# Twenty fused tiles instead of twelve in a talking-heads attention with FFN, opening tiles accumulated in parts

## The chip, the core and the metric

One core of one Trainium2 chip runs the whole program. The metric is the device time of one execution in microseconds (us). Engines are named as in the profile: PE is TensorE, DVE is VectorE, ACT is ScalarE, POOL is GpSimd, SP is SyncE.

## What is computed

Batch 8, 12 heads, sequence 448, head size 64. Attention scores are mixed across heads before the softmax (w_pre) and the weights are mixed across heads after it (w_post); the result, 3584 rows of 768, goes through a feed-forward network of width 2048 with a squared ReLU.

```python
scores = scale * np.matmul(q, k.transpose(0, 1, 3, 2))
scores = np.einsum('bhij,hg->bgij', scores, w_pre)
attn = np.exp(scores - max); attn = attn / (sum + 1e-09)
attn = np.einsum('bhij,hg->bgij', attn, w_post)
x = np.matmul(attn, v)            # then rows of all heads side by side
h = np.maximum(x @ w_in, 0.0)
out = h * h @ w_out
```

## The kernel before

**Tiles.** A tile is ten query rows of one batch with all twelve heads, 120 partitions by 448 keys. A batch has 45 tiles, and one loop of steps (L465) works through 360 of them. In step i, `mix` (L369) makes the mixed scores of tile i on PE, ACT takes the exponential with its row sums, DVE the reciprocal, and POOL scales a 120x120 matrix built from w_post by it (`pn`). Four steps later `unmix` (L392) multiplies the exponentials by that matrix, which mixes the heads and transposes at once, and DVE copies the result to SBUF (L403).

**Two ways to mixed scores.** The usual way has three stages. `score_burst` (L320) computes the scores of 128 queries for a few heads, two matmuls for a pair of heads, and ACT and DVE copy them into a buffer S (two of them, each for a block of 128 queries and all heads). `gather` (L349) then lets SP issue a DMA that brings ten queries of all heads onto 120 partitions (buffer G, twelve of them, at most ten steps ahead). One matmul with the matrix `pre` mixes the heads (L381). For batch 0 there is a second way that needs no gather: the *fused* tiles. `mix_queries` (L172) lets DVE multiply the transposed queries by w_pre for each target head, and six accumulating matmuls of 128x448 per tile (L376), one for each pair of heads, give the mixed scores directly. In the kernel before, tiles 0 to 11 are fused, and tiles 12 to 44 come from three score blocks. The mixed queries are kept in three of the four buffers that later hold w_out.

**The start.** q, k and v of batch 0 are loaded in thirds of four heads (L88 to L94, L426). For each third u, `turn_unit` (L181) transposes q with sixteen small PE transposes, DVE copies them (qT), DVE mixes the queries (tiles 0 to 3 first, then 4 to 11), then k is transposed and ACT copies it (kT). Behind the second third stands a burst for two pairs of heads; the other pairs of the first block follow in steps 0 and 1. Gathers begin in step 2.

**The order of the work.** On PE and POOL instructions keep the order of the program; on DVE and ACT a scheduler chooses the order of the queue. All engines work their queues in order. A PSUM tile is one of eight banks, given out dynamically: a matmul that begins a tile waits until the bank's earlier tile has been copied out. Loads are issued by POOL at fixed steps: `KQ_AT` (k and q of batches 1 and 2), `W1_AT` (w_in in six pieces), `W2_AT` (w_out in eight pieces), `V1_AT`. Transposes of the next batch come at the steps of `TURN`. Between mix and unmix, PE takes units of the feed-forward network from a list (`filler`), as many as spread them evenly to the next bound; `EARLY` (L45) says at which step the hidden units of a third of batch 0 are put on that list.

Of the kernel before, what the change touches and what calls it, by code (L numbers as in the profile page):

```python
# [8 lines left out]
BF16 = mybir.dt.bfloat16  # L9
# [5 lines left out]
B, H, S, D = 8, 12, 448, 64  # L15
DMODEL = H * D
DFF = 2048
NPAIR = H // 2
# [3 lines left out]
IQ = 10  # L22
NT = 45
RG = H * IQ
FUSED = 12
FQ = FUSED * IQ
NEAR = 4
STARTS = {0: (FQ, 2 * FQ, S - 128)}
FIRST = {0: (FUSED, 2 * FUSED, 3 * FUSED)}
BURSTS = {0: ([5, 8], [5, 8], [3, 6])}  # L30
for _b in range(1, B):
    STARTS[_b], FIRST[_b], BURSTS[_b] = (0, 128, 256, 384), (0, 13, 26, 39), ([5, 8], [5, 8], [6], [0, 3])
GATHERS_AT = 2
HALF = H // 2
TT = 15
TQ = TT * IQ
# [1 line left out]
AHEAD = 10  # L38
SCALE = 1.0 / 8.0
TURN = {0: (17, 17, 21, 21, 25, 25), 1: (20, 20, 24, 24, 28, 28), B: (1 + LAG,) * 3 + (16 + LAG,) * 3}  # L40
KQ_AT = {1: (5, 7, 9, 11, 13, 15), 2: (52, 54, 56, 58, 60, 62)}
W1_AT = (-1, 1, 3, 18, 21, 24)
W2_AT = (30, 33, 36, 39, 42, 45, 48, 51)
V1_AT = (47, 50, 53)
EARLY = ((21, 0, 0, 2), (32, 0, 2, 4), (38, 1, 0, 4), (52, 2, 0, 4))  # L45
FFN2_AT = 60
MAIN = 3 * 128

# [2 lines left out]
def kernel(  # L51
# [11 lines left out]
    nc = tc.nc  # L63
    P = nc.NUM_PARTITIONS

    consts = ctx.enter_context(tc.tile_pool(name="consts", bufs=1))
# [12 lines left out]
    def stage_tile(name, bufs):  # L79
        return stage.tile([P, H, R, D], BF16, name=name, tag=name, bufs=bufs)  # L80

    def load(t, src, b, h0=0, h1=H):
        nc.gpsimd.dma_start(out=t[0:PR, h0:h1, :, :].rearrange("p h r d -> p h (r d)"),
                            in_=src[b, h0:h1, :, :].rearrange("h (p r) d -> p h (r d)", r=R))

    staged, vs = {}, {}
    staged[0] = (stage_tile("qst", 1), stage_tile("kst", 1))
# [41 lines left out]
    for t in range(3 * P // IQ, NT):  # L129
        n0, n = max(0, 3 * P - IQ * t), min(IQ, S - IQ * t)  # L130
# [29 lines left out]
    for t in ets:  # L160
# [4 lines left out]
    w2 = [wts.tile([P, FT // 4, DMODEL], BF16, name=f"w2_{x}") for x in range(4)]  # L165

    qTs, kTs, xts, h2ts, ats = {}, {}, {}, {}, {}

    qmix = [w2[u][:, :, :].rearrange("p c m -> p (c m)")[:, 0:2 * FQ * H].rearrange(
        "p (y t g i) -> p y t g i", y=2, g=H, i=IQ) for u in range(NPAIR // 2)]  # L170

    def mix_queries(u, t0, t1):  # L172

        for y in range(2):
            qs = qTs[0][:, 2 * u + y, IQ * t0:IQ * t1].rearrange("p (t i) -> p t i", i=IQ)
            nc.vector.tensor_tensor(out=qmix[u][:, y, t0:t1, :, :],
                                    in0=qs.unsqueeze(2).to_broadcast([P, t1 - t0, H, IQ]),
                                    in1=wrep[:, 2 * u + y, :, :].unsqueeze(1).to_broadcast([P, t1 - t0, H, IQ]),
                                    op=ALU.mult)
# [140 lines left out]
    def score_burst(b, blk, pairs):  # L320
# [3 lines left out]
        sb = Sb[(b, blk)]  # L324
        q0 = STARTS[b][blk]
        got = []
# [22 lines left out]
    def gather(s):  # L349

        b, t = s
        g = work.tile([P, S], BF16, name="G", tag="G", bufs=AHEAD + 2)
        x, end = IQ * t, min(IQ * t + IQ, S)
        while x < end:
            blk = x // P if b else min(x // FQ, 3) - 1
            n = min(end, STARTS[b][blk] + P) - x
            o, y = H * (x - IQ * t), x - STARTS[b][blk]
            sb = Sb[(b, blk)]
            dst = g[o:o + H * n, :]
            if blk < 3:  # L360
                nc.sync.dma_start(out=dst, in_=sb[y:y + n, :, :])
            else:
                for c in range(2):
                    nc.sync.dma_start(out=g[o + HALF * n * c:o + HALF * n * c + HALF * n, :],
                                      in_=sb[64 * c + y:64 * c + y + n, 0:HALF, :])
            x += n
        Gs[s] = g

    def mix(s):  # L369
        n = rows_of(s[1])  # L370
        b, t = s
        ps = bank("m_ps")
        fused = b == 0 and t < FUSED
        if fused:
            for p in range(NPAIR):
                nc.tensor.matmul(ps[0:n, 0:S], rhs=kTs[b][:, p, :],  # L376
                                 lhsT=qmix[p // 2][:, p % 2, t, :, :].rearrange("p g i -> p (g i)"),
                                 start=(p == 0), stop=(p == NPAIR - 1))
        else:
            m = pres[max(x for x in pres if x <= t)] if b else pre  # L380
# [42 lines left out]
    blocks = [(b, blk) for b in range(B) for blk in range(len(STARTS[b]))]  # L423
    steps = [(b, t) for b in range(B) for t in range(NT)]
    with tc.manual_schedule(engines={PE, POOL}):
        for x in range(3):  # L426
            load_v(0, x)
        for u in range(NPAIR // 2):
            turn_unit(0, 0, u)
            mix_queries(u, 0, NEAR)  # L430
            mix_queries(u, NEAR, FUSED)
            turn_unit(0, 1, u, nc.scalar.copy)
            if u == 1:
                score_burst(0, 0, [0, 1])
        loads = {}
        ahead = [FUSED]

# [27 lines left out]
        for i in range(-1, end):  # L465
            for f in loads.get(i, []):
                f()
            if i < 0:
                continue
            if i == NT // 2:  # L470
                for (_, n), (t, order) in orders.items():
                    half_pre(n, t, order)
            s0 = steps[i] if i < len(steps) else None
            s1 = steps[i - LAG] if LAG <= i < len(steps) + LAG else None
            if s0:
                b, t = s0
                if t == 0:
                    if b + 1 < B:
                        for x, u in enumerate(turn_units(b + 1)):
                            at_step(i + TURN.get(b, TURN[B])[x], u)  # L480
            early = [x for x in bounds if x > i]
            rest = early[0] - i if early else (1 + LAG - i) % NT + 1
            rest = min(rest, end - i) if i > len(steps) - NT // 2 else rest
            share = sum(w for w, _ in filler) / rest / 2
            now = timed.pop(i, [])
            if s0:
                mix(s0)
            for w, f in now:
                f()
                owed[0] -= w  # L490
            fill(share)
            if s1:
                unmix(s1)
                b1, t1 = s1
                if t1 % TT == TT - 1:
                    for u in av_units(b1, t1 // TT):
                        at_step(i + 3, u)
                if t1 == NT - 1:
                    at_step(i + 3 if b1 else FFN2_AT, (0, lambda b1=b1: filler.extend(ffn_units(b1))))
            if i < 2:  # L500
                score_burst(0, 0, [2 + 2 * i, 3 + 2 * i])
            for _ in range(2 if i >= GATHERS_AT else 0):
                if ahead[0] > min(max(i + AHEAD, 2 * FUSED - 1), len(steps) - 1):
# [46 lines left out]
```

## Time and profile before

| | |
|---|---|
| three timed runs | 600.27, 600.85 and 602.12 us, median 600.85 |
| the profiled execution | 600.99 us, span 599.2 us |
| busy in the span | PE 574.3, DVE 411.7, ACT 380.6, POOL 326.1 us |
| first matmul | 7.12 us |
| fused mix, 72 matmuls of 128x448 (L376) | tiles 0 to 11, steps 0 to 11 |
| mix of a gathered tile (L381) | 348 matmuls of 120x448, mean 358 ns from start to end |
| gathers | 354 DMA issues by SP |
| read from and written to HBM | 45.70 MB, 11.01 MB |

The mean duration of a matmul reaches from its start to its last result; matmuls overlap, so the distance between two starts is shorter than the duration. A name such as `s_ps L332` is the tile that is written and the line in the kernel before; in the changed kernel the line numbers are higher by up to 35.

### The profile page before, as it was taken

To read this page: it belongs to the slowest core of one execution; us is meant where nothing else is said; L and a number is where in the kernel's file an instruction comes from. 1 tells how busy PE (TensorE), PEld (TensorE's weight loads), DVE (VectorE), ACT (ScalarE), POOL (GpSimd) and SP (SyncE) were. 2 spreads that over 40 slices of the span, in tenths; PEclk is the share of its full clock that TensorE was granted. 3 is DMA by queue.
4 is the path that set the end of the run, shared out by engine and by line. 5 is a ranking of instruction groups with operands and counts; after the bars stand their busy time and mean duration, and the time that the engine had idled before them with its cause. 6 is when DMAs were issued, how large, how long until landed. Compare 5 with 4: busy or idle time off the path is not lost.

```text
span 599.2 us, 17220 instructions
## 1 busy us (share of the span) xinstructions
PE 574.3 (96%) x6011; PEld 372.2 (62%) x6011; DVE 411.7 (69%) x1044; ACT 380.6 (64%) x1105; POOL 326.1 (54%) x708
## 2 busy tenths in 40 slices
PE   4979999899999999999999999999999999999996
PEld 3547777566566666566565665666665666666553
DVE  5668769988767777767777777777867667666011
ACT  3757978676876557864776547775677547762410
POOL 5354897362777227862569316792377325761730
PEclk9999999999999999999999999999999999999999
DMA  9898999698569755795458855697544755431003
GB/s 128 141 199 164 191 197 196 128 172 193 100 101 140 145 100 109 121 156 124 98 94 135 151 111 101 113 143 138 109 79 69 133 119 107 84 50 54 27 27 79
DMA packets 88279, 72.28 MB, mean 121 GB/s; under 512 B 6688, under 2 KB 83200, under 8 KB 88192
## 3 DMA queue, kind: packets, MB, share of 16 engines
q1 hardware_dynamic: 50394, 48.16, 36.6%
q0 software_dynamic: 37216, 22.81, 29.3%
q8 instruction: 47, 0.77, 0.5%
q10 hardware_dynamic: 582, 0.21, 0.2%
q14 instruction: 40, 0.33, 0.1%
HBM read 45.70 MB, written 11.01 MB: 95 GB/s over the span
## 4 chain that ended last, share of the span: by engine, by line
PE 81%; DMA 10%; ACT 3%; issue 2%; DVE 1%; POOL 1%; SPq 1%; ACTq 0%; POOLq 0%; DVEq 0%
PE o_ps L295 24%; PE h_ps L251 22%; PE at_ps L401 10%; PE m_ps L381 10%; DMA G<-S 7%; PE ot_ps L209 6%; PE s_ps L332 4%; PE tr_ps L193 3%; ACT e L384 2%; DMA w<-in_moe_w_in_dram 2%; DMA kst<-in_k_dram 1%; ACT S L342 1%; PE m_ps L376 1%; DVE S L344 1%; PE s_ps L338 1%
## 5 line engine op out<-in xcount | busy, mean ns | idle before, releaser
L403 DVE CAST at<-at_ps 112x480 bf16<-112x480 f32 x360 | 228.5, 650 | 73.3 <-PE at_ps L401 72.8
L384 ACT ACTIVATE e<-m_ps 120x448 bf16<-120x448 f32 x360 | 195.5, 547 | 98.8 <-PE m_ps L381 92.4
L388 POOL TENSOR_SCALAR pn<-post,rc 120x120 bf16<-120x120 bf16 x348 | 129.0, 372 | 207.1 <-DVE rc L386 147.6
L251 PE MATMUL h_ps<-xt,w 128*128 128x448 bf16 (+2 forms) x960 | 169.6, 315 | 1.1 <-ACT hr L257 0.6
L295 PE MATMUL o_ps<-w,h 128*128 128x384 bf16 x768 | 138.7, 326 | 0.3 <-ACT S L342 0.2
L401 PE MATMUL at_ps<-pn,e 120*128 120x120 bf16 (+1 forms) x1440 | 135.1, 216 | 0.7 <-POOL pn L388 0.5
L401 PEld LDWEIGHTS <-e 120*128 120x128 bf16 (+1 forms) x1440 | 103.9, 98 | 45.0 <-issue 1.4
L381 PE MATMUL m_ps<-G,pre 120*120 120x448 bf16 x348 | 124.6, 358 | 2.1 <-ACT S L342 1.0
L251 PEld LDWEIGHTS <-w 128*128 128x128 bf16 x960 | 84.6, 98 | 57.7 <-issue 5.6
L262 POOL TENSOR_TENSOR h<-hr 128x384 bf16<-128x384 f32 (+1 forms) x144 | 106.1, 738 | 19.4 <-ACT hr L257 15.6
L257 ACT ACTIVATE hr<-h_ps 128x448 f32<-128x448 f32 (+2 forms) x160 | 75.4, 473 | 52.7 <-PE h_ps L251 35.9
L295 PEld LDWEIGHTS <-h 128*128 128x128 bf16 x768 | 72.8, 98 | 48.2 <-issue 5.5
L344 DVE CAST S<-s_ps 128x448 bf16<-128x448 f32 x159 | 89.2, 615 | 4.2 <-DMA G<-S 2.3
L386 DVE RECIPROCAL rc<-sm 120x1 f32<-120x1 f32 x360 | 57.2, 159 | 45.2 <-ACT e L384 37.3
L342 ACT CAST S<-s_ps 128x448 bf16<-128x448 f32 x171 | 79.8, 546 | 11.9 <-PE s_ps L332 8.4
L384 ACT ACTIVATION_READ_ACCUMULATOR e<-m_ps 120x1 f32 x360 | 74.1, 206 | 0.0
L304 DVE COPY osb<-o_ps 128x384 f32<-128x384 f32 x54 | 30.1, 557 | 46.8 <-PE o_ps L295 46.6
L381 PEld LDWEIGHTS <-pre 120*120 120x120 bf16 x348 | 46.1, 133 | 20.9 <-issue 14.6
L332 PE MATMUL s_ps<-kT,qT 64*128 64x448 bf16 x288 | 41.5, 355 | 5.8 <-ACT S L342 4.4
L209 PE MATMUL ot_ps<-at,v 112*64 112x150 bf16 x1152 | 42.6, 230 | 0.0
L209 PEld LDWEIGHTS <-v 112*64 112x64 bf16 x1152 | 38.3, 110 | 4.9 <-issue 4.9
L215 ACT CAST xt<-ot_ps 128x450 bf16<-128x450 f32 (+1 forms) x48 | 25.5, 533 | 20.4 <-PE ot_ps L209 19.9
(45 smaller groups left out, 288.2 us busy)
## 6 DMA issues: line engine op xcount, KB each, us to landing
G<-S SPq DMA_DIRECT2D x284, 105.0 KB
qst<-in_q_dram POOLq DMA_DIRECT2D x24, 224.0 KB, 5.7
kst<-in_k_dram POOLq DMA_DIRECT2D x24, 224.0 KB, 5.2
v<-in_v_dram POOLq DMA_DIRECT2D x24, 224.0 KB, 6.9
G<-S SPq DMA_DIRECT2D x70, 52.5 KB
w<-in_moe_w_in_dram POOLq DMA_DIRECT2D x6, 512.0 KB, 10.3
w<-in_moe_w_out_dram POOLq DMA_DIRECT2D x8, 384.0 KB, 7.7
out_dram<-osb SPq DMA_DIRECT2D x8, 336.0 KB
```

The costliest lines, as they stand in the source:

```text
L209: nc.tensor.matmul(ps[64 * hh:64 * hh + 64, TQ * y:TQ * y + TQ], lhsT=vs[b][0:PR, g, r, :], rhs=at[0:PR, r, g, :], start=(y == 0 and r == ...
L251: nc.tensor.matmul(ps[:, 0:n], lhsT=w1[ft // 8][:, c2, ft % 8 * 128:ft % 8 * 128 + 128], rhs=xts[b][:, c2, n0:n1], start=(c2 == 0), stop=( ...
L257: nc.scalar.activation(out=hr[:, 0:n], in_=ps[:, 0:n], func=ACT.Relu)
L262: eng.tensor_tensor(out=dst[:, x - o:y - o], in0=hr[:, x - n0:y - n0], in1=hr[:, x - n0:y - n0], op=ALU.mult)
L295: nc.tensor.matmul(ps[:, 0:384], lhsT=lhsT, rhs=w2[ft // 4][:, ft % 4, nt * 384:(nt + 1) * 384], start=(ft == 0), stop=(ft == FT - 1))
L342: nc.scalar.copy(out=sb[:, h, :], in_=ps[:, 0:S])
L344: nc.vector.tensor_copy(out=sb[:, h, :], in_=ps[:, 0:S])
L381: nc.tensor.matmul(ps[0:n, 0:S], lhsT=m[0:n, 0:n], rhs=Gs.pop(s)[0:n, :], start=True, stop=True)
L384: nc.scalar.activation(out=e[0:n, 0:S], in_=ps[0:n, 0:S], func=ACT.Exp, scale=SCALE, accum_out=sm[0:n, 0:1])
L388: nc.gpsimd.tensor_scalar(out=pn[0:n, :], in0=(post_gi if fused else post)[0:n, :], scalar1=rc[0:n, 0:1], scalar2=1.0, op0=ALU.mult, op1=A ...
L401: nc.tensor.matmul(ps[:, RG * r:RG * r + RG], lhsT=e[0:n, PR * r:PR * r + P], rhs=pn[0:n, :], start=True, stop=True)
L403: nc.vector.tensor_copy(out=ats[(b, third)][0:PR, :, :, IQ * tl:IQ * tl + IQ], in_=ps[0:PR, 0:R * RG].rearrange("p (r g i) -> p r g i", r= ...
```

## The change

Twenty tiles are fused instead of twelve. Two score blocks remain in batch 0 (queries 200 to 327 and 320 to 447) instead of three. The mixed queries of tiles 12 to 19 go to three more buffers that are free at that time: the fourth one of w_out, the second one of v and the second one of the FFN's input (`late`); their mixing is written at steps 3, 4 and 5, one third each. For tiles 0 to 4 the six accumulating matmuls are issued in three parts of two (`fused_part`): the part of a third of the heads follows the transposes of the next third's q, and the last part stands in the tile's own step. Thirteen matmuls on a zeroed tile (`still`) stand ahead of the first transposes, two more behind the first k. The first score block moves from the start to steps 0 to 2, gathers begin in step 4, and the steps of some loads and of one `EARLY` entry move. Buffers are computed from the same data, and nothing else of the computation changes.

In the queues of the built program, PE has 86 more rows, the DMA issues of SP are eight fewer, and from about step 39 on all five queues are the same as before. DVE's scheduled queue has the mixing for tiles 12 to 19 at the start: one of the six instructions stands ahead of the second third's mixing, three behind it and ahead of the third q copy, two behind the third third's mixing, and only then come the first reciprocal and the score copies.

```diff
-FUSED = 12
+FUSED = 20
+SOON = 12
-NEAR = 4
-STARTS = {0: (FQ, 2 * FQ, S - 128)}
-FIRST = {0: (FUSED, 2 * FUSED, 3 * FUSED)}
-BURSTS = {0: ([5, 8], [5, 8], [3, 6])}
+NEAR = 5
+STARTS = {0: (FQ, S - 128)}
+FIRST = {0: (FUSED, 32)}
+BURSTS = {0: ([4, 8], [5, 8])}
-GATHERS_AT = 2
+GATHERS_AT = 4
+WARM = (13, 2)
-KQ_AT = {1: (5, 7, 9, 11, 13, 15), 2: (52, 54, 56, 58, 60, 62)}
-W1_AT = (-1, 1, 3, 18, 21, 24)
+KQ_AT = {1: (4, 6, 8, 10, 12, 14), 2: (52, 54, 56, 58, 60, 62)}
+W1_AT = (-1, 1, 3, 15, 17, 19)
-EARLY = ((21, 0, 0, 2), (32, 0, 2, 4), (38, 1, 0, 4), (52, 2, 0, 4))
+EARLY = ((21, 0, 0, 2), (28, 0, 2, 4), (38, 1, 0, 4), (52, 2, 0, 4))
...
+    still_in = consts.tile([P, 512], BF16, name="still_in")
+    nc.vector.memset(still_in[:, :], 0.0)
+    still_out = bank("still_ps")
+
+    def still(n):
+        for _ in range(n):
+            nc.tensor.matmul(still_out[:, :], lhsT=still_in[:, 0:P], rhs=still_in[:, :], start=True, stop=True)
...
+    late = [w2[3][:, :, :].rearrange("p c m -> p (c m)"), stage_tile("v", 2)[:, :, :, :].rearrange("p h r d -> p (h r d)"),
+            ffnp.tile([P, NPAIR, S], BF16, name="xt", tag="xt", bufs=2)[:, :, :].rearrange("p c s -> p (c s)")]
+
+    def mixed(u, y, t0, t1):
+        if t0 < SOON:
+            buf, x = w2[u][:, :, :].rearrange("p c m -> p (c m)"), SOON * y + t0
+        else:
+            buf, x = late[u], (FUSED - SOON) * y + t0 - SOON
+        return buf[:, RG * x:RG * (x + t1 - t0)]
...
+    parts = {}
+
+    def fused_part(t, u):
+
+        if t not in parts:
+            parts[t] = [0, bank("m_ps")]
+        if parts[t][0] > u:
+            return
+        parts[t][0] = u + 1
+        for p in (2 * u, 2 * u + 1):
+            nc.tensor.matmul(parts[t][1][0:RG, 0:S], rhs=kTs[0][:, p, :], lhsT=mixed(u, p % 2, t, t + 1),
+                             start=(p == 0), stop=(p == NPAIR - 1))
...
         if fused:
-            for p in range(NPAIR):
-                nc.tensor.matmul(ps[0:n, 0:S], rhs=kTs[b][:, p, :],
-                                 lhsT=qmix[p // 2][:, p % 2, t, :, :].rearrange("p g i -> p (g i)"),
-                                 start=(p == 0), stop=(p == NPAIR - 1))
+            for u in range(NPAIR // 2):
+                fused_part(t, u)
+            ps = parts[t][1]
...
+        still(WARM[0])
         for x in range(3):
             load_v(0, x)
         for u in range(NPAIR // 2):
             turn_unit(0, 0, u)
             mix_queries(u, 0, NEAR)
-            mix_queries(u, NEAR, FUSED)
+            mix_queries(u, NEAR, SOON)
+            if u:
+                for t in range(NEAR):
+                    fused_part(t, u - 1)
             turn_unit(0, 1, u, nc.scalar.copy)
-            if u == 1:
-                score_burst(0, 0, [0, 1])
+            if u == 0:
+                still(WARM[1])
...
-            if i < 2:
-                score_burst(0, 0, [2 + 2 * i, 3 + 2 * i])
+            if 2 < i < 6:
+                mix_queries(i - 3, SOON, FUSED)
+            if i < 3:
+                score_burst(0, 0, [2 * i, 2 * i + 1])
```

More of the change, by code (lines that the diff above doesn't have):

```diff
@@ L167 @@
     qTs, kTs, xts, h2ts, ats = {}, {}, {}, {}, {}
-    qmix = [w2[u][:, :, :].rearrange("p c m -> p (c m)")[:, 0:2 * FQ * H].rearrange(
-        "p (y t g i) -> p y t g i", y=2, g=H, i=IQ) for u in range(NPAIR // 2)]
+    late = [w2[3][:, :, :].rearrange("p c m -> p (c m)"), stage_tile("v", 2)[:, :, :, :].rearrange("p h r d -> p (h r d)"),
[6 more added lines that the diff above has]
+        return buf[:, RG * x:RG * (x + t1 - t0)]
     def mix_queries(u, t0, t1):
@@ L175, in mix_queries @@
             qs = qTs[0][:, 2 * u + y, IQ * t0:IQ * t1].rearrange("p (t i) -> p t i", i=IQ)
-            nc.vector.tensor_tensor(out=qmix[u][:, y, t0:t1, :, :],
+            nc.vector.tensor_tensor(out=mixed(u, y, t0, t1).rearrange("p (t g i) -> p t g i", g=H, i=IQ),
                                     in0=qs.unsqueeze(2).to_broadcast([P, t1 - t0, H, IQ]),
@@ L354, in gather @@
         while x < end:
-            blk = x // P if b else min(x // FQ, 3) - 1
+            blk = max(y for y, q0 in enumerate(STARTS[b]) if q0 <= x)
             n = min(end, STARTS[b][blk] + P) - x
@@ L371, in mix @@
         b, t = s
-        ps = bank("m_ps")
         fused = b == 0 and t < FUSED
         if fused:
-            for p in range(NPAIR):
-                nc.tensor.matmul(ps[0:n, 0:S], rhs=kTs[b][:, p, :],
-                                 lhsT=qmix[p // 2][:, p % 2, t, :, :].rearrange("p g i -> p (g i)"),
-                                 start=(p == 0), stop=(p == NPAIR - 1))
+            for u in range(NPAIR // 2):
+                fused_part(t, u)
+            ps = parts[t][1]
         else:
+            ps = bank("m_ps")
             m = pres[max(x for x in pres if x <= t)] if b else pre
@@ L499 @@
                     at_step(i + 3 if b1 else FFN2_AT, (0, lambda b1=b1: filler.extend(ffn_units(b1))))
-            if i < 2:
-                score_burst(0, 0, [2 + 2 * i, 3 + 2 * i])
+            if 2 < i < 6:
+                mix_queries(i - 3, SOON, FUSED)
+            if i < 3:
+                score_burst(0, 0, [2 * i, 2 * i + 1])
             for _ in range(2 if i >= GATHERS_AT else 0):
-                if ahead[0] > min(max(i + AHEAD, 2 * FUSED - 1), len(steps) - 1):
+                if ahead[0] > min(max(i + AHEAD, FIRST[0][1] - 1), len(steps) - 1):
                     break
```

## The prediction

> **What bounds the kernel now.** I read the page first: TensorE (PE) is busy nearly all the time, and the chain that ended last is PE's for four fifths.
>
> ```profile
> span 599.2 us, 17220 instructions
> PE 574.3 (96%) x6011; PEld 372.2 (62%) x6011; DVE 411.7 (69%) x1044; ACT 380.6 (64%) x1105; POOL 326.1 (54%) x708
> PEclk9999999999999999999999999999999999999999
> ```
>
> So a change can gain only where PE stands still or runs slowly, and each matmul that it adds costs its full length. Busy shares hide slow matmuls, so I took the starts of all matmuls from the trace and used the median distance from one start to the next as a matmul's price: 189 ns for a fused one (128x448), 192 ns for the mix of a gathered tile, 52 ns for one of an unmix, 190 ns for a pair of score matmuls (they start together). Time minus the sum of prices is loss. Up to 68.72 us, where step 38 begins, the loss is 25.2 us; behind that it is 11.5 us up to step 109 and then about 1 us per 50 us. The view by stretches, the timeline and the waits name the early ones (columns of the stretches: PE, PEld, DVE, ACT, POOL busy, granted clock, DMA share, GB/s):
>
> ```profile
> 35.00:40.00 5.00, 4.75 (x70) 2.96 (x68) 4.88 (x16) 4.11 (x16) 4.42 (x11) 1.00 1.10 194
> 40.00:45.00 5.00, 1.44 (x9) 0.76 (x6) 2.63 (x7) 1.88 (x5) 1.01 (x3) 0.92 1.16 208
> 45.00:50.00 5.00, 5.00 (x96) 4.20 (x95) 2.73 (x7) 2.52 (x7) 1.49 (x3) 0.74 0.89 175
> ```
>
> ```profile
> 39.27 0.96 PE L332 MATMUL s_ps<-kT,qT 64*128 64x448 bf16 x5
> 43.71 0.35 PE L332 MATMUL s_ps<-kT,qT 64*128 64x448 bf16 x1 [3.47 <-ACT S L342]
> ```
>
> ```profile
> PE s_ps L332 <- ACT S L342: 4.4, 3, 3.5
> ```
>
> PE stands still for 3.47 us in the third score block of batch 0. The page names ACT's copy; the chain shows what ACT waited for: the score buffer is still being read by the gathers of the first block.
>
> ```profile
> 33.60 9.42 DMA G<-S
> 43.02 0.02 issue
> 43.04 0.04 ACTq L342
> ```
>
> Behind the stall the granted clock drops; what the two stretches miss, (0.08 + 0.26) x 5 us, is 1.7 us of PE lost. The start loses 7.12 us until the first load lands and 6.9 us more until step 5 at 23.87 us, in part because the first matmuls take twice as long:
>
> ```profile
> 15.03 2.24 PE L376 MATMUL m_ps<-kT,w 128*120 128x448 bf16 x6
> 17.68 1.35 PE L376 MATMUL m_ps<-kT,w 128*120 128x448 bf16 x6
> ```
>
> **Work added and removed.** Eight more fused tiles: 8 x (6 x 0.189 - 0.192) = +7.54 us. One score block of twelve matmuls less: 6 pairs x 0.19 = -1.14 us. Net +6.40 us of PE time, with no cover anywhere, since PE is the bound.
>
> **Stall and clock.** The third block's buffer wait goes with the block (-3.47), the low clock behind it (-1.7), and about 0.5 us that its second half costs at 49.76 us beyond its matmuls: -5.7 us. What could be late next at that place is the gather of tiles 20 to 31. They are issued at step 4, about 23.4 us, when the last score copy is done; twelve at 0.77 to 1.2 us of SP each are out by 36 us, and with the 9.4 us that the chain shows for one landing they are in by 45.2 us, when step 20 mixes the first. The next block (batch 1) needs that buffer at step 27. Nine us of cover or so; if it were gone, PE would wait a gather's 9.4 us at most.
>
> **The start.** The transposes begin at 7.12, 9.29, 10.47 and 11.64 us as their loads land (issue plus 5.7 to 8.2 us); the last two loads land at 12.8 and 13.95. These times do not move. The thirteen matmuls on zeros, 512 columns, cost 0.427 us each at half speed (0.373 x 512/448), so they end at about 6.6 us at the latest, before the first load: nothing on the path. The two more stand between landings at 9.29 and 10.47: nothing at full clock, 0.4 us at half.
>
> Twenty of the thirty matmuls of tiles 0 to 4 now run between the transposes. With PE at full clock: k of the first third is copied by ACT (0.91 us) at 10.8; ten matmuls take 1.89 us, to 12.74; two units of transposes, then ACT's copy of the second k ends at 14.25; ten more to 16.2; transposes, and the third k copy ends at 17.75. DVE must be ready as well. Its rows:
>
> ```profile
> L176 DVE TENSOR_TENSOR w<-qT,wrep 128x960 bf16<-128x960 bf16 x6 | 3.7, 653 | 0.0
> L176 DVE TENSOR_TENSOR w<-qT,wrep 128x480 bf16<-128x480 bf16 x6 | 2.2, 405 | 0.1
> ```
>
> Started one behind the other they stand 0.57 and 0.326 us apart, so 600 elements take 0.387 and 840 take 0.509: a third still costs 1.79 us. But DVE's queue in the changed kernel holds the mixing for tiles 12 to 19 here, not at steps 3 to 5 where it is written: 6 x 0.57 = 3.4 us, of which four (2.28 us) stand ahead of the third q copy. The first q copy stands at 8.73, behind an instruction that waits for a load of w_post until 8.53, and stays there. 8.73 + 0.655 + 1.79 + 0.655 + 1.79 + 2.28 + 0.655 + 0.77 = 17.3 us for the last mix that tile 0 needs. So the added DVE work uses up the slack under the k copy (17.75), and tile 0 ends at 18.2, against 17.2 now. Then a new wait: five of the eight PSUM banks hold open tiles, and each burst of four scores waits for ACT's copies (0.424 us apart) and exponentials (0.534) of the burst before. Queued behind are all mixes and unmixes. From 18.35: one exponential, four copies, to 20.6; the second burst ends at 20.9, the third at 22.0; the ends of tiles 3 and 4 (0.76) and an unmix (0.21) bring step 5 to 22.95 us. Now it is at 23.87 with half of the second block (0.57) done: 23.30. The start gains 0.35 us where the moved matmuls alone would be worth 3.8 us.
>
> **Steps 5 to 38.** Fifteen fused steps of 1.134 + 0.208 = 1.342 us, two bursts of 0.67 (as at 23.20 and 26.70), one pair of transposes 0.78: step 20 at 45.2 us, against 44.14. From there to step 38 PE now takes 24.58 us for 19.13 us of matmuls. Without the low clock (1.7), the second half of the removed block (0.57) and its 0.5 this is 21.8 us: step 38 at 67.0 us. DVE gives a later bound. From 42.3 us it has 21 unmix copies at 0.65, 21 reciprocals at 0.1 (0.07 to 0.15 from start to start), 6 transposed copies at 0.655, 3 small copies (0.55) and 6 score copies at 0.57: 23.6 us, and with the 2 us or so that it idles in such stages step 38 comes at 67.8 to 68.3 us. I take 68.1, DVE's, because it was at 5.00 of 5 us from 55 to 60 us. By then one hidden unit of FFN more (0.39 us) has been issued. 68.72 - 68.1 + 0.39 = 1.0 us gained; by PE's bound 2.1 us.
>
> **Moved at no cost.** The loads of k and q for batch 1 come one step earlier and those of w_in three to five steps: POOL issues each in 0.74 us, behind it the normalisations (0.37 us) needed four steps later; in a fused step of 1.34 us both fit. Without that cover a step would lengthen by 0.74 us. The last w_in load is asked for at 44 instead of 53.41 us and removes the 0.24 us wait for it at 63.4. Three groups of hidden units move from step 32 to 28: same number. From step 39 on all engines' queues are the same in both kernels.
>
> **Sum.** Work +6.40; stall, clock and block -5.7; start -0.35; steps 5 to 20 lose 2.1 us now beside the stall (the 0.4 us steps 12 to 19, transposes among them) and 0.2 then, -1.9; steps 20 to 38 lose 3.25 us now beside clock and block (24.58 - 19.13 - 1.7 - 0.5) and 3.8 then, +0.55. Together -1.0 us. The profiled run took 600.99 us for a span of 599.2, the median shown is 600.85: 600.99 - 1.0 = 600.0 us.
>
> **A rule against it.** About 0.5 us of matmuls at the end of the 3.47 us stall did not keep the clock up, as the stretches show. The Trainium skill (TensorE: Matmul & The Clock Gate, Part 1: The HAM clock gate, and Part 4: PE-mode transpose) says that the clock falls after an idle window of about 3.4 us, that these windows run freely, and that transposes do not count as activity. By that rule only the two zero matmuls could hold the clock between the thirteen and the first parts, and where a window misses them the time is that of the second rival below. The trace leaves it open: here the first matmuls at full speed come at 16.9 us, behind transposes and matmuls without a gap.
>
> **Rivals.** *Faster:* DVE's backlog is absorbed and PE's own bound holds: 600.99 - 2.1 = 598.9, 598 if idle time in the stage shrinks too. For it: DVE idles 1.6 to 2.4 us of each 5 between 20 and 35 us, so it enters step 20 with none owed. Against: seven unmix copies cost it 5 us while PE needs 2.8.
> *Slower: the clock is down again when the parts start.* Each of the 20 part matmuls at 0.373 costs 0.184 us more, and they stand on the path to the k copies. Seven of them cost 1.3 us (601.3); from 15 on (2.7 us and more) the kernel is slower by over 0.3%, and all 20 give 603.7. For it: the twenty stand alone between transposes, and the first six fused ones were slow in the same place. Against: thirteen zero matmuls ahead of them.
> *Evacuation stage:* eight hidden units now crowd steps 26 and 27, ahead of a score burst whose banks they hold; POOL squares one in 0.43 us and waits its turn behind a normalisation that DVE's queue delays. POOL then needs 8 x 0.43 + 3 x 0.37 = 4.55 us where PE needs 8 x 0.39 + 2 x 0.40 = 3.9: 0.65 us; if each of the two score bursts holds back the unmix copies by DVE's three score copies (1.7 us) as well, 4.1: 600.7 to 604.1, in the middle 602.4.
> *That it doesn't do what it says:* the block cannot stall if it is gone; but a gather later than 45.2 us would bring the stall back at step 20. The chain's 9.4 us leaves cover; I count it into the last case.
>
> **Chances.** Forecast 0.36, faster 0.28, clock 0.22 and evacuation 0.14, each of the latter two half within 0.3% and half beyond. 0.3% (1.8 us) is about what a measurement can tell from no change. Faster 0.28, same 0.36 + 0.11 + 0.07 = 0.54, slower 0.18. The range reaches from the faster rival's lower end, 598, to 602.9 in the slower ones.
>
> **What would show it.** Step 5 at 23.0 us; part matmuls 0.19 us apart (0.37 tells of the slow clock); no stall near 40 us and a granted clock of 1.00 from 35 to 50; step 20 at 45 and step 38 at 68 us; the same losses behind. A wait of PE for gathers at step 20, or a start later than 24.5 us, would prove me wrong.

## The result and the profile after

The changed kernel takes 604.75 us (median of five runs, 604.14 to 605.22) beside 601.30 us for the kernel before (600.27 to 602.29); the ratio is 1.0059, interval [1.0036, 1.0081]. It is slower, by about 3.5 us, and lies above the range of the forecast. The profiled execution took 604.75 us for a span of 602.7 us. The first lines of its page:

```profile
span 602.7 us, 17274 instructions
PE 585.0 (97%) x6054; PEld 376.2 (62%) x6054; DVE 413.4 (69%) x1047; ACT 377.4 (63%) x1097; POOL 326.6 (54%) x708
PEclk8999999999999999999999999999999999999999
```

PE is busy 10.7 us longer. The added work is 6.4 us of that by the prices of the prediction, and the fifteen matmuls on zeros are busy for another 6.3 us, thirteen of them before the first load lands. The other rows together fell by 2.0 us, the transposes most.

```profile
L94 PE MATMUL still_ps<-still_in 128*128 128x512 bf16 x15 | 6.3, 599 | 1.2 <-DVE still_in L89 1.2
```

So the busy time does not tell where the loss is. The clock tells a part: an 8 now stands in its first slice. The view by stretches says where it is low (columns as in the prediction):

```profile
7.00:10.00 3.00, 1.47 (x34) 0.98 (x34) 2.02 (x8) 0.26 (x1) 2.09 (x4) 1.00 1.30 171
10.00:14.00 4.00, 3.95 (x27) 2.47 (x26) 3.94 (x9) 0.65 (x1) 0.07 (x1) 0.57 1.45 196
35.00:40.00 5.00, 5.00 (x39) 3.57 (x37) 2.78 (x8) 2.19 (x8) 2.67 (x6) 1.00 1.01 180
40.00:45.00 5.00, 5.00 (x65) 3.62 (x63) 2.35 (x8) 2.54 (x8) 3.45 (x7) 1.00 1.12 180
45.00:50.00 5.00, 5.00 (x84) 3.96 (x85) 4.32 (x13) 2.32 (x8) 2.21 (x6) 1.00 1.11 190
115.00:120.00 5.00, 2.76 (x33) 1.52 (x34) 4.74 (x12) 2.21 (x6) 2.10 (x5) 0.96 0.34 72
120.00:125.00 5.00, 5.00 (x29) 2.90 (x29) 1.78 (x6) 1.68 (x6) 0.79 (x3) 0.70 0.70 109
```

From 35 to 50 us PE stands full at a clock of 1.00: the stall and the low clock of before are gone. In their place are two stretches of half clock, from 10.38 and from 119.60 us, each 3.41 us long in the trace, so 1.7 us of PE each. The timeline of PE shows the first: the clock fell behind the two zero matmuls and the transposes, and ten part matmuls took 3.40 us where the ten of the next third took 2.05.

```profile
9.63 0.61 PE L94 MATMUL still_ps<-still_in 128*128 128x512 bf16 x2
10.29 0.91 PE L210 MATMUL tr_ps<-ident,qst 112*64 112x112 bf16 x16
11.13 3.40 PE L396 MATMUL m_ps<-kT,w 128*120 128x448 bf16 x10
...
16.04 2.05 PE L396 MATMUL m_ps<-kT,w 128*120 128x448 bf16 x10 [0.61 <-ACT kT L212]
```

Step starts (first matmul of the tile's mix, us), the quickest way to see where the time went:

| step | 5 | 20 | 38 | 62 | 80 | end of span |
|---|---|---|---|---|---|---|
| before | 23.87 | 44.14 | 68.72 | 101.55 | 125.01 | 599.16 |
| forecast | 22.95 | 45.2 | 68.1 | 100.5 | 124.0 | 598.2 |
| after | 24.94 | 47.82 | 68.99 | 101.59 | 128.51 | 602.72 |

(The forecast's entries behind step 38 are the times before less the 1.0 us of its sum.) At step 62 the two kernels are level, where the forecast had a gain of 1.0 us. Then, in a stage where all five queues hold the same instructions, the changed kernel loses 3.46 us between steps 62 and 80, and behind that nothing more. PE's waits between 100 and 125 us, before and then after (total, times, longest):

```profile
PE tr_ps L193 <- DMA qst<-in_q_dram: 1.1, 1, 1.1
PE s_ps L332 <- ACT S L342: 0.4, 1, 0.4
```

```profile
PE s_ps L349 <- ACT S L359: 1.5, 1, 1.5
PE tr_ps L210 <- DMA qst<-in_q_dram: 1.2, 1, 1.2
```

The wait for a score copy grew by 1.1 us, and the chain of waits of the changed kernel tells what the copy waited for: gather behind gather, 21.0 of the 25.7 us from 93.69 to 119.39 us. (From 85 to 125 us gathers are 52.5% of this chain, 24.3% in the kernel before.)

```profile
93.69 9.94 DMA G<-S
103.62 0.02 issue
103.64 0.02 SPq L378
103.66 0.03 issue
103.69 6.35 DMA G<-S
...
113.72 4.71 DMA G<-S
118.43 0.53 ACT S L359
118.96 0.04 issue
119.00 0.39 PE s_ps L349 x2
```

SP's own queue says the same. Between 60 and 120 us it waited for gathers to land before it could issue the next ones, first before, then after:

```profile
SPq L361 <- DMA G<-S: 0.6, 1, 0.6
```

```profile
SPq L378 <- DMA G<-S: 10.0, 20, 1.6
```

After 1.2 us without q and 1.5 us without a score buffer, with transposes and a few matmuls between them, the clock drops at 119.60 us, as it did behind the stall at 40 us in the kernel before.

What moved the gathers? The loads of w_out are asked for at steps 30 to 51 in both kernels, but step 30 now comes at 60.81 instead of 58.10 us, and POOL issues the first w_out load at 62.7 instead of 59.1 us, while the last w_in load has landed by 56.6 us (63.35 before). The queue table between 55 and 65 us (packets, MB, share of the DMA engines; q0 holds POOL's loads, q1 SP's gathers), before and after:

```profile
q0 software_dynamic: 498, 0.86, 65.5%
q1 hardware_dynamic: 790, 0.65, 22.5%
```

```profile
q1 hardware_dynamic: 1135, 0.94, 44.8%
q0 software_dynamic: 19, 0.03, 6.0%
```

For some 6 us the load queue is empty, and then eight w_out loads must pass in 25.4 us instead of 29 us, with the loads of v, k and q of later batches right behind them.

Only the first four are squeezed, though: they are issued within 8.6 us instead of 11.9, and from the fifth on the w_out loads are issued within 0.5 us of those of the kernel before and land with them (the last at 97.08 us, 97.27 before). The gathers carry the delay on. Those that SP issues between 77 and 85 us in the kernel before come 2.6 to 4.3 us later in the changed one. So nine instead of six of 105 KB are issued between 85 and 95 us, where POOL's loads take 91% of the DMA engines' time (95% before). Queue and gathers from 85 to 95 us, before and after:

```profile
q0 software_dynamic: 1830, 1.41, 94.6%
G<-S SPq DMA_DIRECT2D x6, 105.0 KB
```

```profile
q0 software_dynamic: 1693, 1.37, 90.6%
G<-S SPq DMA_DIRECT2D x9, 105.0 KB
```

The gather bytes that are issued but not yet moved, worked out from the trace's DMA packets, then stand at about 0.4 to 0.5 MB from 87 to 108 us, against 0.2 to 0.4 MB before, and at 114 us still at 0.29 MB against 0.12. The repeated profiles of both kernels (r2 and r1 below) show the same picture.

### The profile page after: what moved, and what is told of

The parts are those of the page before. It is cut to its first block, busy times and chain, and to the rows that moved or that the text cites. A ratio compares the mean times of both kernels' runs of the same rounds, so it can differ in the third digit from the quotient of the medians.

```text
span 602.7 us, 17274 instructions
## 1 busy us (share of the span) xinstructions
PE 585.0 (97%) x6054; PEld 376.2 (62%) x6054; DVE 413.4 (69%) x1047; ACT 377.4 (63%) x1097; POOL 326.6 (54%) x708
## 4 chain that ended last, share of the span: by engine, by line
PE 86%; DMA 6%; ACT 4%; issue 1%; POOL 1%; DVE 1%; ACTq 0%; POOLq 0%; DVEq 0%; SPq 0%
PE o_ps L312 24%; PE h_ps L268 23%; PE at_ps L430 11%; PE m_ps L410 10%; PE ot_ps L226 6%; DMA G<-S 5%; PE m_ps L396 4%; PE s_ps L349 4%; PE tr_ps L210 3%; ACT S L359 2%; ACT e L413 1%; DMA qst<-in_q_dram 1%; PE s_ps L355 1%; POOL h L279 1%; DVE at L432 0%
## 5 line engine op out<-in xcount | busy, mean ns | idle before, releaser
L417 POOL TENSOR_SCALAR pn<-post,rc 120x120 bf16<-120x120 bf16 (+1 forms) x340 | 127.0, 375 | 202.8 <-DVE rc L415 147.6
L410 PE MATMUL m_ps<-G,pre 120*120 120x448 bf16 (+1 forms) x340 | 121.7, 358 | 2.1 <-ACT S L359 1.0
L361 DVE CAST S<-s_ps 128x448 bf16<-128x448 f32 x155 | 86.8, 615 | 2.8 <-PE s_ps L349 1.5
L359 ACT CAST S<-s_ps 128x448 bf16<-128x448 f32 x163 | 76.4, 548 | 9.2 <-PE s_ps L349 7.8
L410 PEld LDWEIGHTS <-pre 120*120 120x120 bf16 (+1 forms) x340 | 45.1, 133 | 17.7 <-issue 10.9
## 6 DMA issues: line engine op xcount, KB each, us to landing
G<-S SPq DMA_DIRECT2D x70, 52.5 KB
```

The lines of the kernel that those rows point to most:

```text
L359: nc.scalar.copy(out=sb[:, h, :], in_=ps[:, 0:S])
L361: nc.vector.tensor_copy(out=sb[:, h, :], in_=ps[:, 0:S])
```

## Experiments

Theory A: the loss has two parts, the low clock at the start and the w_out loads that come too late and crowd the gathers of steps 62 to 79. Rivals: the loss comes from the parts or the zero matmuls themselves (B); from moving w_in, k and q early (C); or it is spread of a kernel that loses clock at random (D). The measured numbers of all runs stand in one table; each kernel was timed against the kernel before on its own chip. "Lost clock" is (1 - mean granted clock) x span, a mean over the executions of that kernel; 0.3 to 1.0 us of it lie at the very end of every profile. Steps are of the profiled execution.

| run | us | ratio to before | lost clock | step 20 | 62 | 62 to 80 | half clock from (us) |
|---|---|---|---|---|---|---|---|
| r1_before | 601.13 | 0.9982 [0.9960, 1.0005] | 3.8 | 44.08 | 101.82 | 23.15 | 44.07 |
| r2_after | 605.10 | 1.0066 [1.0043, 1.0088] | 5.5 | 47.63 | 101.39 | 26.96 | 10.28, 119.51 |
| e1_nozero | 605.20 | 1.0062 [1.0041, 1.0082] | 3.7 | 47.60 | 101.42 | 25.44 | 115.52 |
| e2_noparts | 604.48 | 1.0039 [1.0020, 1.0059] | 6.7 | 48.02 | 101.73 | 28.10 | 9.19 (10.2 long), 118.41 (6.8) |
| e3_w2early | 602.47 | 1.0019 [0.9993, 1.0045] | 3.7 | 48.21 | 100.70 | 25.28 | 10.97, 116.79 |
| e4_hold | 604.13 | 1.0040 [1.0024, 1.0057] | 3.3 | 46.97 | 100.69 | 26.98 | 118.95 |
| e8_w2_hold | 600.73 | 0.9988 [0.9965, 1.0011] | 2.2 | 46.82 | 99.36 | 23.58 | none |
| e13_zeros_w2 | 601.47 | 0.9996 [0.9967, 1.0025] | 2.2 | 47.26 | 101.13 | 23.62 | none |
| e12_w2first_hold | 601.43 | 0.9996 [0.9966, 1.0026] | 2.1 | 46.96 | 100.31 | 25.24 | 116.74 |
| e9_oldsteps | 603.06 | 1.0032 [1.0009, 1.0056] | 3.5 | 47.75 | 101.92 | 25.17 | 9.59, 118.82 |
| e10_w2late | 603.28 | 1.0045 [1.0020, 1.0071] | 4.8 | 43.11 | 100.57 | 26.64 | 43.66, 118.75 |
| e5_loads | 603.04 | 1.0021 [0.9999, 1.0043] | 3.4 | 48.15 | 102.23 | 24.94 | 9.76, 118.99 |
| e6_loads_hold | 602.27 | 1.0014 [0.9992, 1.0036] | 2.0 | 47.10 | 101.18 | 24.84 | 117.36 |
| e7_before_loads | 611.03 | 1.0150 [1.0126, 1.0175] | 8.5 | 41.38 | 109.19 | 24.56 | 42.80, 56.45 (10.2 long), 124.72 |
| e11_old_hold_w2 | 608.33 | 1.0100 [1.0070, 1.0131] | 3.8 | 47.24 | 109.68 | 23.56 | 77.81 (6.8 long) |

(The mean times behind step 80 differ by the same amount as there. A profiled execution can lie some 2 us off its kernel's median, as in e1 and e8; the median decides.)

**Both kernels again.** 

> The kernel before, unchanged, once more. It tells how much of the late difference is of the kernel and how much of the execution. Theory A (the score copy's wait for gathers at 116 to 119 us and the clock drop behind it come and go from one execution to the next, in both kernels): this profile has them, losing 1.5 to 3.5 us between steps 62 and 80 against the first profile. Theory B (they belong to the changed kernel): the score copy waits 0.2 us again, no clock drop at 115 to 123 us, and the ratio is 1.000.

> The changed kernel, unchanged, once more, beside the same runs of the kernel before as the next three. Theory (its loss is of the kernel): ratio 1.004 to 1.007, and in the profile again a half-speed stretch near 10 to 14 us or a later start, and again a score copy's wait for gathers of about 1 us at 116 to 119 us with a clock drop behind it. If the ratio falls to 1.002 or less, the first measurement had caught unlucky executions.

(The letters A and B in the first of these are its own.) The kernel before measured against itself gives 0.9982, the changed kernel again 1.0066, with its two half-clock stretches at the same places to 0.1 us. The loss belongs to the kernel; D falls as the whole cause. In r1's profile PE waits 1.2 us for a score copy as well (0.4 in the first profile of the kernel before), but not for q, and the clock stays up: 23.15 us from step 62 to 80. One such wait is therefore part of the kernel before too, and a wait of that size alone need not lose the clock. Single executions of the kernel before still spread from 598.3 to 605.4 us, so one execution tells little here.

**The start: zero matmuls and parts.** Without the zero matmuls:

```diff
-WARM = (13, 2)
+WARM = (0, 0)
```

> The changed kernel without its fifteen matmuls on zeros. Theory of the clock (the zero matmuls raise it at 7 us, but it falls back from 10.4 to 13.8 us, so they buy little): the clock rises once, at 13 to 17 us, the parts run 0.37 us apart at first, step 5 begins between 24.5 and 26 us (24.94 in the changed kernel), total within 1 us of the changed kernel's 604.75. Rival (they already buy much): step 5 after 27 us and the total 2 us or more above it.

Measured 605.20 us. The ten first parts took 2.96 us, a little less than with the zero matmuls (3.40), and step 20 comes 0.2 us earlier: the zero matmuls as placed bought nothing that these runs can tell.

Without the early parts (the six matmuls of tiles 0 to 4 all in the tile's step):

```diff
-            if u:
-                for t in range(NEAR):
-                    fused_part(t, u - 1)
```

> The changed kernel with tiles 0 to 4 accumulated in one piece in their own steps. Theory (the parts move 3.8 us of matmuls, but bursts then wait for banks and copies): step 5 later by 0 to 1.5 us than 24.94, total 604.5 to 606.5. Rival (the parts cost time, by the banks that they hold and the waits that they put in front of the k transposes): step 5 before 24.5 us and the total under 604.

Measured 604.48 us, no better beyond the noise. The start then runs 10.2 us at half clock, with even less between the transposes, and step 20 is only 0.2 us later than with parts. Neither undoing helps, so B falls as the main cause: each of these edits is nearly neutral, and the loss is elsewhere.

Holding the clock instead, with five more zero matmuls behind the first q transposes and four instead of two behind the first k:

```diff
-WARM = (13, 2)
+WARM = (13, 4)
...
+            if u == 0:
+                still(5)
```

> The changed kernel with seven more matmuls on zeros, five between the first q and k transposes and two more behind the first k, so that PE is never idle long before the parts. Theory of the clock: no slow stretch from 10 to 14 us, part matmuls 0.19 us apart, step 5 at 23 to 23.7 us instead of 24.94; the total 1 to 1.5 us below the changed kernel (603.3 to 603.8) if what the start gains reaches the end, and unchanged (604.7) if POOL's and the loads' bound between steps 40 and 79 takes it back. Rival: the clock falls again, step 5 at 24.9 or later.

```profile
11.57 2.10 PE L396 MATMUL m_ps<-kT,w 128*120 128x448 bf16 x10
13.61 0.58 PE L210 MATMUL tr_ps<-ident,kst 112*64 112x112 bf16 x16
```

The ten parts start 0.44 us later, behind the longer zeros, and take 2.10 us; step 5 comes at 24.09 instead of 24.94 us and the 0.85 us last to step 62 (100.69 against 101.59). The time falls only to 604.13 us, which the intervals do not tell from the changed kernel's, and steps 62 to 80 still take 26.98 us. So the clock at the start is a small part at most, and the late loss does not come from it.

**The late stage: w_out.** The loads of w_out eight steps earlier, alone and with the held clock:

```diff
-W2_AT = (30, 33, 36, 39, 42, 45, 48, 51)
+W2_AT = (22, 25, 28, 31, 34, 37, 40, 43)
```

> The changed kernel with the eight loads of w_out asked for eight steps earlier (steps 22 to 43 instead of 30 to 51). Theory of the load order (the w_in loads were moved forward, the w_out loads were not and come 3.6 us later in time, DMA is half idle from 55 to 65 us, then the loads crowd the gathers, and a score copy at 118 us waits for gathers): steps 66 to 79 no longer lose 3.45 us against the kernel before, granted clock 1.00 from 115 to 125 us, total 600.5 to 602. Rival (the late stall has nothing to do with the w_out loads): it stays, total 604 to 605.5.

> The changed kernel with the w_out loads eight steps earlier and seven more matmuls on zeros at the start. Both effects together: w_out early gave 2.2 us, the held clock 0.85 us up to step 62; total 601 to 602 against 604.7 of the changed kernel, and level with the kernel before. If the two do not add up (POOL or the gathers bind behind step 40), as with w_out early alone: 602 to 603.

Alone it takes the time to 602.47 us: the wait for q at 114 us is gone, but a wait of 1.2 us for score copies and a half-clock stretch behind it stayed, so only the time, not the clock, came near its expectation. With the held clock it takes 600.73 us, 4.4 us below the changed kernel on the same chip and level with the kernel before. Its waits between 60 and 120 us: SP waited for gathers 3.9 us instead of 10.0, PE 0.9 us for a score copy, not at all for q. Its gather bytes outstanding are down to about 0.15 MB at 108 us (0.53 in the changed kernel). This run and e4 differ in the steps of w_out alone: 604.13 against 600.73 us, with intervals that do not meet, and 26.98 against 23.58 us from step 62 to 80. The clock stays up:

```profile
115.00:120.00 5.00, 4.75 (x39) 2.82 (x38) 4.55 (x13) 2.54 (x9) 2.45 (x5) 1.00 0.69 92
120.00:125.00 5.00, 4.67 (x70) 3.32 (x68) 4.33 (x12) 3.96 (x12) 2.32 (x6) 1.00 0.85 159
```

The other direction, in the kernel before, which has no parts, no zeros and its old loads otherwise: the first six w_out loads two steps later, the seventh one step.

```diff
-W2_AT = (30, 33, 36, 39, 42, 45, 48, 51)
+W2_AT = (32, 35, 38, 41, 44, 47, 49, 51)
```

> The kernel before with the loads of w_out two steps later, which is about the time at which the changed kernel asks for them (62 instead of 59 us). If the time of the w_out loads makes the late stall, this kernel gets it too: score copy's wait for gathers of 1 us or more at 116 to 119 us, total 602 to 604. If not: 601 to 601.8, as the kernel before.

```profile
PE tr_ps L193 <- DMA qst<-in_q_dram: 1.6, 1, 1.6
PE s_ps L332 <- ACT S L342: 1.2, 1, 1.2
```

603.28 us. POOL issues the first w_out load at 61.7 us, and the late loss appears in the kernel before: both waits (ACT's score copy stands 1.3 us behind gathers), a half-clock stretch at 118.75 us, 26.64 us from step 62 to 80. No other part of the change is in this run. Together with e4 and e8, where w_out alone moves the other way, it shows that late w_out loads make a late loss. It costs 1.9 us here (601.35 us for the kernel before on that chip), about half of the changed kernel's 3.8. The path is not the same one: the last w_in load lands at 61.32 us, so the load queue has hardly a gap. SP doesn't wait long for landings (10.0 us in the changed kernel, 7.1 in r2). Instead the loads themselves stand closer, at 97.8% of the DMA engines' time from 85 to 95 us.

**The moved w_in, k and q (rival C).** The changed kernel with these loads and the `EARLY` entry at their steps of before:

```diff
-KQ_AT = {1: (4, 6, 8, 10, 12, 14), 2: (52, 54, 56, 58, 60, 62)}
-W1_AT = (-1, 1, 3, 15, 17, 19)
+KQ_AT = {1: (5, 7, 9, 11, 13, 15), 2: (52, 54, 56, 58, 60, 62)}
+W1_AT = (-1, 1, 3, 18, 21, 24)
...
-EARLY = ((21, 0, 0, 2), (28, 0, 2, 4), (38, 1, 0, 4), (52, 2, 0, 4))
+EARLY = ((21, 0, 0, 2), (32, 0, 2, 4), (38, 1, 0, 4), (52, 2, 0, 4))
```

> The changed kernel with the old steps for the loads of k and q of batch 1 and of w_in, and the old step 32 for the second group of hidden units. Theory (the moved w_in loads leave DMA idle from 55 to 65 us, and what is behind crowds the gathers): the stall at 118 us shrinks, total 602 to 603.5. Rival (the moved loads are harmless, the late loads come late because step 30 comes late): 604 to 606, as the changed kernel or worse.

603.06 us, 2.0 us below the changed kernel on the same chip (the intervals overlap). With hidden units back at step 32, step 30 comes at 58.39 us, and w_out is issued from 61.0 us, behind the later w_in, not from 62.7. SP's gather waits fall to 1.8 us and the late stage to 25.17 us, of which a half-clock stretch still takes its 1.7. C holds in part, as far as the noise lets one say: the moved steps took part of the time. With the old steps the load queue has no gap of 6 us.

**All loads early.** w_out, then v and the k and q of batch 2, six to eight steps earlier, in the changed kernel, with the held clock, and in the kernel before:

```diff
-KQ_AT = {..., 2: (52, 54, 56, 58, 60, 62)}
-W2_AT = (30, 33, 36, 39, 42, 45, 48, 51)
-V1_AT = (47, 50, 53)
+KQ_AT = {..., 2: (46, 48, 50, 52, 54, 56)}
+W2_AT = (22, 25, 28, 31, 34, 37, 40, 43)
+V1_AT = (39, 42, 45)
```

> The changed kernel with the loads of w_out eight steps, of v for batch 1 eight steps and of k and q for batch 2 six steps earlier. Theory of the loads (all of them together crowd the gathers at 95 to 118 us): neither the 1.2 us wait for q at 113 us nor the score copy's wait for gathers at 118 us is left, no clock drop there, total 600 to 601.5, against 604.75. Rival (the gathers are slow by themselves): the wait of the score copy stays at 1 us or more and the total at 602.5 or above.

> The same, with seven more matmuls on zeros at the start, which kept the clock up in an earlier run (step 20 came 0.85 us earlier). If the late stage no longer binds, the 0.85 us reach the end: 0.5 to 1 us below the kernel with the loads alone. If POOL and the loads still bind between steps 40 and 79, no difference.

> The kernel before with the same loads moved by the same steps. If the late stall is a matter of the loads alone, this gains too: 599 to 600.5 against 601.2, and the two kernels with moved loads then differ by what the fused tiles are worth by themselves, within 1 us. If the kernel before has no such stall to lose, its total stays within 0.5 us, 600.7 to 601.7.

In the changed kernel, 603.04 and 602.27 us: no better than with w_out alone, and above what was expected of the loads. The load queue is nearly idle between 105 and 115 us, and still a half-clock stretch fell behind the transposes and the score burst. In the kernel before, which needs its gathers from step 12 on, the same edit costs 9 us, where a gain or no change was expected. ACT's waits from 40 to 130 us:

```profile
ACT S L342 <- DMA G<-S: 11.2, 3, 8.7
```

So early loads are not free either: there they stand in front of gathers that are due, and 10.2 us of half clock follow.

**Where w_out should start.** All three with the held clock; e11 also has w_in, k, q and `EARLY` at their steps of before.

```diff
+W2_AT = (26, 28, 31, 34, 37, 40, 43, 46)   # e11
+W2_AT = (20, 22, 25, 28, 31, 34, 37, 40)   # e12
+W2_AT = (26, 29, 32, 35, 38, 41, 44, 47)   # e13
```

> The changed kernel with the loads of k, q and w_in and the EARLY entry at their steps of before, five zero matmuls behind the first q transposes and four behind the first k, and w_out asked for at steps 26, 28, 31 ... 46 instead of 30 ... 51. If the late loss hangs on when the last POOL load is out (w_out), whatever the order of w_in: no wait of 1.2 us for score copies near 117 us, no half-speed window before the last 10 us, step 62 near 100.0 us, step 76 near 118 us, 600.5 to 601.5 us. If w_in at its old steps pushes w_out back behind the gathers again: waits of 1 us and more near 115 us and a half-speed window, 602 to 603.5 us.

> The changed kernel with the zero matmuls (five more behind the first q transposes, four behind the first k) and w_out asked for at steps 20, 22, 25 ... 40. If an earlier w_out only helps: step 62 near 99.2 us, step 76 near 117 us, no half-speed window before the last 10 us, 600 to 600.7 us, below the kernel before by 0.1 to 0.2%. If w_out now runs beside the gathers that steps 20 to 31 wait for: a wait for gathers at step 20 or behind it, step 38 later than 68.5 us, 602 us or more.

> The changed kernel with the same zero matmuls and w_out asked for at steps 26, 29 ... 47, halfway between the run with steps 22 to 43 (600.73 us) and the one with steps 30 to 51 (604.13 us). If the loss grows with each step that w_out comes later: step 76 near 119 us, 601.5 to 602.5 us. If there is a point up to which it costs nothing (the gathers' ten-step lead absorbs it): step 76 near 117.4 us and 600.5 to 601 us.

e13 and e12 take 601.47 and 601.43 us, level with the kernel before and with e8 within what the measurement tells. From step 20 to step 26 the start of w_out makes no difference that I can measure. The numbers of e13 fit the first of its expectations (step 76 at 119.18 us), but e12, with w_out six steps earlier, is no faster. e12 met neither of its expectations. Its profile has a half-clock stretch at 116.74 us and those of e8 and e13 have none; PE waited 0.9 us for a score copy in all three, and what made the difference is not shown. e11 missed both of its expectations: 608.33 us. Its late stage is fine (23.56 us), but between 55 and 65 us the last two w_in loads and the first three w_out loads fill the queue, and a gather issued at 64.22 us landed 14.38 us later:

```profile
q0 software_dynamic: 851, 1.40, 86.5%
q1 hardware_dynamic: 617, 0.52, 18.0%
```

```profile
64.08 0.14 PE m_ps L410
64.22 14.38 DMA G<-S
78.61 0.02 issue
```

PE waited 5.1 us for the score copy behind it and then ran 6.8 us at half clock. This is the third place (after e7 and the late stage) where POOL's loads beside due gathers set the time. The Trainium skill (DMA: Bandwidth & Descriptors, Queues, rings and completion order) says that each DMA engine takes turns between the queues it has work for, packet by packet. The rows agree in direction, though they do not show the turns: in the ten us with q0 at 86.5% of the engines' time q1 moved 0.52 MB, where it moved 0.94 MB beside a nearly empty q0, and the gather issued at the end of them took 14.38 us.

No version beat the kernel before by more than the measurement tells. e8 is the best at 0.9988 [0.9965, 1.0011].

## Why the prediction was wrong, step by step

- **Work added, +6.40 us.** Not contradicted: later tiles' fused matmuls stand 189 ns apart as priced, and the counts hold.
- **Stall, clock and block, -5.7 us.** Right in its mechanism (its size by itself was not measured). No wait for score copies and no low clock from 35 to 50 us; no wait for gathers at step 20, so the rival "doesn't do what it says" falls.
- **The start, -0.35 us.** Wrong: step 5 came at 24.94, not 22.95 us. The second rival happened: the clock was down for most of the first ten of the twenty parts. It had 0.22 of the chance. Its price was right (ten parts in 3.40 instead of 2.10 us, 1.3 us as for seven slow ones); e4 got 0.85 us of it back at step 5, because its longer zeros put the parts off by 0.44 us. The other 0.7 us are errors of the working: the parts start at 11.13 instead of 10.8 us, the last third starts 0.2 us later behind them than priced, and the bursts with five open banks take 0.14 us more. The thirteen zero matmuls ended at 6.93 us, not 6.6, and still ahead of the first transposes. By the rule of the Trainium skill (TensorE: Matmul & The Clock Gate, Part 1) the clock falls after an idle window of about 3.4 us. The row agrees if transposes count for little: the clock went up at 6.96 us behind the thirteen zero matmuls and fell 3.41 us later, at 10.38 us, and of the 1.80 us that PE was busy in between, 0.61 were the two zero matmuls and the rest transposes. The late drop at 119.60 us does not fit the rule as it stands, since PE was busy for 1.61 of the 3.41 us ahead of it.
- **Steps 5 to 20.** 22.88 us instead of 22.25: 0.6 us too little.
- **Steps 20 to 38.** 21.17 us where I took DVE's bound, 22.9, over PE's, 21.8. The mechanism of the *Faster* rival holds here: DVE's backlog never reached PE. This gave back 1.7 us, so that step 38 came at 68.99 us, 0.9 behind the forecast.
- **Evacuation stage.** Did not happen: steps 26 to 38 took 14.99 us against 15.52 before.
- **"The same losses behind" and "Moved at no cost".** This is the step that failed most: +3.46 us where I had nothing, and no rival covered it. I had priced the moved loads by POOL's 0.74 us of issue and by the w_in wait that went, and had taken equal queues behind step 39 for equal times. What stays at its step also moves when its step comes later: the w_out loads began 3.6 us later behind an empty queue, and the first four passed in less time. The gathers beside them fell behind and into the loads of the next batches, the wait for a score copy grew from 0.4 to 1.5 us, close behind the wait for q, and the clock went down for 3.41 us. That the time of the w_out loads makes the loss is shown by e8 against e4 and, in the kernel before, by e10; the path from them to the clock is read from the traces.

The terms add up: against the forecast +1.99 (start), +0.63, -1.73, +0.2 (steps 38 to 62), +3.46 and 0.06 behind, together 4.6 us, which is the span of 602.72 less the 598.16 forecast.

What stays open: of the 3.46 us, about 1.7 are the half-clock stretch, and whether a given execution has it is not settled by the waits ahead of it. The lost clock over all executions (5.5 us after, 3.8 before, 2.2 in e8) says that it is no accident of one trace, but the split between waits and clock is only known to about 1 us. Why e8, without stalls, is no faster than the kernel before is also not settled: over its executions it loses 1.5 us less clock than that kernel on its chip, and its mean time without the lost clock is 1.3 us higher.

## What to carry to other kernels

Price a moved load by the queue it leaves and the queue it enters, not by its issue: bytes that leave an empty stretch in a load queue can stand beside transfers that are due later on. When the queues of two kernels are equal from some step on, ask at what time that step comes and which transfers hang on it. A few dummy matmuls need not hold the clock (two among the first transposes did not here, nine did); look at the granted clock where the work starts, not where the dummies stand.

## What the runs showed of the hardware

In these traces the granted clock is full or half. From its first rise on it changes only after whole multiples of 3.41 us: 8 of them at full clock before the drop at 44.18 us in the kernel before, 31 between the two half-clock stretches of the changed one. A half-clock stretch lasts 3.41 us (or twice or three times that), and each 3.41 us cost 1.7 us when PE has work. Thirteen zero matmuls of 0.427 us raised the clock at 6.96 us; two more did not keep it; seven more beside those two (five behind the first q transposes, two behind the first k) kept it in the profiles of e4, e6, e8, e11, e12 and e13.

Late in the kernel no threshold shows. Behind waits of 2.7 us together (changed kernel), 2.8 us (e10), 1.2 us (e3), 0.9 us (e12) and 0.8 us (e9) the clock dropped; behind 1.5 us (first profile of the kernel before), 1.2 us (r1) and 0.9 us (e8, e13) it did not. PE's busy time in the 3.41 us ahead does not decide either: 1.61 us in the changed kernel and 2.34 us in e9 came before a drop, and 1.98 us in r1 (115.75 to 119.16 us) did not. What does is open.

The lost clock goes with the spread of executions, but is not all of it: 132 executions of the kernel before range from 598.3 to 607.4 us, at mean clocks of 0.997 down to 0.988, and with the lost clock taken off they still range from 595.3 to 601.2 us.
